# A linear-attention layer and a Fourier mixer on one core: transposes on TensorE, heads in pairs, and Fourier transforms folded in half

## The chip, the cores and the metric

The kernel runs on one core of a Trainium2 chip. The metric is the device time of one execution in microseconds (us). The kernel before took 419.92 us in the median of three runs (419.65 to 425.19).

The engines are named as in the profile: PE is TensorE (PEld its weight loads), DVE is VectorE, ACT is ScalarE, POOL is GpSimd, and SP is SyncE, which here only issues DMAs. PSUM is the memory that TensorE writes.

## The reference

```
# attention: B=4, H=8 heads, S=768 steps, D=48; state is D x D for each head
for t in range(S):
    cur      = outer(u * k[t], v[t])
    y[t]     = r[t] @ (state + cur)
    state    = w[:, None] * state + outer(k[t], v[t])
x = y with the heads side by side                      # B x 768 x 384
# mixer
mixed = real(fft(fft(x, axis=1), axis=2))              # along the sequence, then along the 384 channels
u_    = x + mixed
un    = (u_ - mean(u_)) / sqrt(var(u_) + 1e-6)         # over the 384 channels
out   = u_ + relu(un @ w_ch1) @ w_ch2                  # 384 -> 1536 -> 384
```

## The kernel before, in words

The sequence of a batch is cut into six chunks of 128 steps. Decay powers are folded into r and k (r times w to the power of the position, k times its inverse), so that inside a chunk the attention is two products and a mask: A = k r^T, masked by a triangle (`MA`), then y = MA^T v plus r times the state. The state is 48 x 48 for each head and goes from chunk to chunk.

`phase1_pro(b)` prepares a whole batch. It loads k and r by head on SP's queue and v on ACT's queue, in pieces of 128 x 6 x 48. For each head it scales six chunks at once on DVE (L162, L167) and turns them around by a DMA transpose (L164, L169: r and k, 32 transposes each in the kernel). The term with u (`T1`, `DELTA`, `TTALL`, L171 to L178) is made on DVE for the whole batch in five operations of 2,304 elements a partition.

`phase1_loop(b)` runs over the six chunks: eight matmuls A of one head each (L207, 48 rows of the array), two mask multiplies (L210), sixteen matmuls y (L224 and L227), eight state updates (L233), and on DVE the decay of the state (L239, L242) and the eviction of y into `XSBb` (L244).

`phase2(b)` is the mixer. The transform along the sequence is 12 groups of six matmuls of 384 columns (L274: six row blocks, cosine and sine), each evicted on ACT (L277) and transposed by DMA (L283). The transform along the channels is six groups of six matmuls (L291, L294). For each row block DVE adds x (`UF`, L296) and takes statistics (L297, L298); then one square root and one reciprocal for all six blocks (L300, L301), six normalisations (`UN`, L304), and six DMA transposes (L308). The two layers of the MLP follow: 72 matmuls (L314) with ReLU on ACT (L317), 72 matmuls (L321), and on DVE the residual (`osb`, L324), stored by SP (L325).

The order on each engine is set by a scheduler of the framework, which takes the program in the order in which it is written, with tile pools that say how many buffers each name has, and mixes independent work. The program order is attention 0, tables and weights, and then, for b = 1 to 3, `phase1_pro(b)`, `phase2(b-1)`, `phase1_loop(b)`, and last `phase2(3)`. Each engine runs its own list in order and waits by semaphores for the others.

Of the kernel before, what the change touches and what calls it, by code (L numbers as in the profile page):

```python
# [9 lines left out]
AluOp = mybir.AluOpType  # L11
Act = mybir.ActivationFunctionType
AX = mybir.AxisListType

B = 4
H = 8
# [5 lines left out]
NC = S // L  # L22
DP = 64
# [3 lines left out]
def kernel(  # L27
# [7 lines left out]
    moe_w_ch1: bass.AP,  # L35
    moe_w_ch2: bass.AP,
    out: bass.AP,
    debug: dict | None = None,
    subset: str | None = None,
):  # L40
    nc = tc.nc
    debug = debug or {}

    def dbg_store(name, src_ap):
        if name not in debug:
            return
        dst = debug[name]
        if dst.dtype == src_ap.dtype:
            nc.sync.dma_start(out=dst, in_=src_ap)
        else:  # L50
            nc.gpsimd.dma_start(out=dst, in_=src_ap)
# [12 lines left out]
    _cs_np = np.cos(2.0 * np.pi * np.outer(_n, _n) / S).astype(np.float32)
    _ss_np = np.sin(2.0 * np.pi * np.outer(_n, _n) / S).astype(np.float32)
    _d = np.arange(DM)
    _cd_np = np.cos(2.0 * np.pi * np.outer(_d, _d) / DM).astype(np.float32)
    _nsd_np = (-np.sin(2.0 * np.pi * np.outer(_d, _d) / DM)).astype(np.float32)
    _cs_l = _cs_np.reshape(6, 128, S).transpose(1, 0, 2).astype(mybir.dt.np(mybir.dt.bfloat16))
    _ss_l = _ss_np.reshape(6, 128, S).transpose(1, 0, 2).astype(mybir.dt.np(mybir.dt.bfloat16))  # L70
    _cd_l = _cd_np.reshape(3, 128, DM).transpose(1, 0, 2).astype(mybir.dt.np(mybir.dt.bfloat16))
    _nsd_l = _nsd_np.reshape(3, 128, DM).transpose(1, 0, 2).astype(mybir.dt.np(mybir.dt.bfloat16))
    _mtri_l = _mtri_np.astype(mybir.dt.np(mybir.dt.bfloat16))
    cs_c = nc.inline_tensor(np.ascontiguousarray(_cs_l), name="cs_c")
    ss_c = nc.inline_tensor(np.ascontiguousarray(_ss_l), name="ss_c")
    cd_c = nc.inline_tensor(np.ascontiguousarray(_cd_l), name="cd_c")
    nsd_c = nc.inline_tensor(np.ascontiguousarray(_nsd_l), name="nsd_c")
    mtri_c = nc.inline_tensor(np.ascontiguousarray(_mtri_l), name="mtri_c")
    cs_t = constp.tile([128, 6, S], mybir.dt.bfloat16, name="cs_t")
    ss_t = constp.tile([128, 6, S], mybir.dt.bfloat16, name="ss_t")  # L80
    cd_t = constp.tile([128, 3, DM], mybir.dt.bfloat16, name="cd_t")
    nsd_t = constp.tile([128, 3, DM], mybir.dt.bfloat16, name="nsd_t")
    mtri = constp.tile([128, 128], mybir.dt.bfloat16, name="mtri")
    nc.sync.dma_start(out=mtri, in_=mtri_c.ap())
    def load_big_tables():
        for nb in range(6):
            nc.sync.dma_start(out=cs_t[:, nb, :], in_=cs_c.ap()[:, nb, :])
            nc.sync.dma_start(out=ss_t[:, nb, :], in_=ss_c.ap()[:, nb, :])
        for nb in range(3):
            nc.sync.dma_start(out=cd_t[:, nb, :], in_=cd_c.ap()[:, nb, :])  # L90
            nc.sync.dma_start(out=nsd_t[:, nb, :], in_=nsd_c.ap()[:, nb, :])
    dbg_store("dbg_cst0", cs_t[:, 0, 0:256])
    dbg_store("dbg_cdt0", cd_t[:, 0, 0:256])

    wrow = buildp_obj.tile([128, H, D], mybir.dt.float32, name="wrow")
    nc.sync.dma_start(out=wrow, in_=w.partition_broadcast(128))
    urow = constp.tile([128, H, D], mybir.dt.float32, name="urow")
    nc.scalar.dma_start(out=urow, in_=u.partition_broadcast(128))
    lw = buildp_obj.tile([128, H, D], mybir.dt.float32, name="lw")
    nc.scalar.activation(lw, wrow, Act.Ln)  # L100
    tmp_wp = buildp_obj.tile([128, H, D], mybir.dt.float32, name="tmp_wp")
    wpp = constp.tile([128, H, D], mybir.dt.bfloat16, name="wpp")
    wpn = constp.tile([128, H, D], mybir.dt.bfloat16, name="wpn")
    wpl = constp.tile([128, H, D], mybir.dt.bfloat16, name="wpl")
    nc.vector.tensor_scalar(out=tmp_wp, in0=lw, scalar1=icol[:, 0:1], scalar2=None, op0=AluOp.mult)
    nc.scalar.activation(wpp, tmp_wp, Act.Exp)
    ncol = buildp_obj.tile([128, 1], mybir.dt.float32, name="ncol")
# [27 lines left out]

    if subset == "phase0":
        return

    XSB = []

    def bq(tab):
        return tab.unsqueeze(2).to_broadcast([128, H, NC, D])

# [235 lines left out]
```

## Time and profile before

| | |
|---|---|
| median of three runs | 419.92 us |
| span of the profiled execution (first to last instruction) | 417.7 us |
| mean granted TensorE clock | 0.837 |
| busy PE / DVE / ACT / POOL | 289.8 / 189.8 / 85.2 / 44.5 us |
| first of the 72 first-layer matmuls of batch 0 | 134.15 us |
| last eviction `osb` of batch 3 | 414.23 us |
| DMA packets, of these under 512 bytes | 166,342, 158,000 |

The profile gives no other time for the profiled execution than its span. The median of the runs is 2.2 us above the span.

In a row of the windows view stand the stretch, its length, then busy time and number of instructions of PE, PEld, DVE, ACT and POOL, the granted clock, the DMA engines' busy share and GB/s. In a row of the chain or the timeline stand start, length, engine and operation. In a row of a group stand line, engine, operation, tiles, shapes and count, then busy time and the mean ns of one, then the idle time before it and what ended that.

### The profile page before, as it was taken

The page shows a single profiled execution, that of the slowest core. Times are in us where ns is not written, and L with a number is a line of the kernel's source. Part 1 is how long each engine was busy: PE and PEld are TensorE (multiplying, and loading weights), DVE is VectorE, ACT ScalarE, POOL GpSimd, SP SyncE. Part 2 cuts the span into 40 slices and gives each one's busy share as a digit, 9 for nine tenths or more (in the row PEclk, how much of TensorE's full clock was granted, in tenths as well). Part 3 has the DMA queues.
Part 4 walks back from the last instruction along what each step waited for, and adds up shares of the span by engine and source line. Part 5 has one row for each costly group of instructions (what it writes and reads, how often), then busy time and mean ns, then how long its engine had stood idle before and what let it go on. Part 6 is the DMA issues. An engine that isn't in the chain of part 4 may idle for free. (4 is left out here: it accounts for less than half of the span.)

```text
span 417.7 us, 4723 instructions
## 1 busy us (share of the span) xinstructions
PE 289.8 (69%) x1712; PEld 160.9 (39%) x1712; DVE 189.8 (45%) x326; ACT 85.2 (20%) x161; POOL 44.5 (11%) x95
## 2 busy tenths in 40 slices
PE   0000189885275999865777999866758999982796
PEld 0000046442043556532345456433334565550453
DVE  0244865754565923764168714733571135035012
ACT  3300000312000460211200550320104600220460
POOL 2524400111110000121100000211000000000000
PEclk9999999988585699788755799788866995797799
DMA  8999999355796002466894002547320020131002
GB/s 183 231 192 193 257 224 230 87 118 112 148 220 139 13 19 96 79 135 133 165 189 100 16 36 79 119 105 132 61 48 11 19 96 0 39 75 40 17 20 94
DMA packets 166342, 44.59 MB, mean 107 GB/s; under 512 B 158000, under 2 KB 166320, under 8 KB 166320
## 3 DMA queue, kind: packets, MB, share of 16 engines
q1 hardware_dynamic: 137664, 37.02, 40.7%
q10 hardware_dynamic: 25632, 4.92, 6.2%
q0 software_dynamic: 3024, 2.36, 4.0%
q8 instruction: 13, 0.21, 0.2%
q14 instruction: 9, 0.07, 0.0%
HBM read 22.25 MB, written 4.72 MB: 65 GB/s over the span
## 5 line engine op out<-in xcount | busy, mean ns | idle before, releaser
L314 PE MATMUL pfnA<-UNT,W1SB 128*128 128x384 bf16 x288 | 65.9, 364 | 19.2 <-DMA UNT<-UN 19.2
L207 PE MATMUL A_ps<-RWT,KWT 48*128 48x128 bf16 x192 | 25.3, 270 | 63.0 <-DMA KWT<-KWNh 59.8
L317 ACT ACTIVATE HT<-pfnA 128x384 bf16<-128x384 f32 x96 | 47.1, 491 | 62.1 <-PE pfnA L314 60.8
L321 PE MATMUL pfnB<-W2SB,HT 128*128 128x384 bf16 x288 | 56.3, 331 | 0.0
L324 DVE TENSOR_TENSOR osb<-pfnB,UF 128x384 f32<-128x384 f32 x24 | 13.4, 558 | 83.6 <-PE pfnB L321 82.0
L314 PEld LDWEIGHTS <-W1SB 128*128 128x128 bf16 x288 | 29.8, 106 | 47.9 <-issue 34.0
L274 PE MATMUL pfnA<-XSBb,cs_t 128*128 128x384 bf16 x144 | 39.0, 401 | 12.3 <-ACT t3sb L277 9.7
L274 PE MATMUL pfnA<-XSBb,ss_t 128*128 128x384 bf16 x144 | 39.7, 403 | 10.6 <-ACT t3sb L277 10.6
L277 ACT CAST t3sb<-pfnA 128x384 bf16<-128x384 f32 x48 | 22.5, 478 | 109.8 <-PE pfnA L274 34.4
L207 PEld LDWEIGHTS <-KWT 48*128 48x128 bf16 x192 | 15.5, 116 | 70.9 <-DMA KWT<-KWNh 61.5
L210 DVE TENSOR_TENSOR MA<-A_ps,mtri 128x512 bf16<-128x512 f32 x48 | 32.7, 682 | 21.4 <-PE y_ps L224 18.9
L224 PE MATMUL y_ps<-VALL,MA 128*128 128x48 bf16 x192 | 36.5, 211 | 5.2 <-DVE XSBb L244 3.8
L321 PEld LDWEIGHTS <-HT 128*128 128x128 bf16 x288 | 28.2, 99 | 20.0 <-issue 1.4
L294 PE MATMUL pfnB<-nsd_t,T3ST 128*128 128x384 bf16 x72 | 29.0, 403 | 8.0 <-DMA T3ST<-t3sb 8.0
L227 PE MATMUL y_ps<-SALL,RWT 48*128 48x48 bf16 x160 | 33.7, 211 | 0.0
L291 PE MATMUL pfnB<-cd_t,T3CT 128*128 128x384 bf16 x72 | 28.5, 396 | 4.6 <-DVE STS L297 4.6
L166 POOL MEMSET KWNh<- 128x480 bf16 x32 | 15.9, 497 | 144.6 <-DMA KWT<-KWNh 143.5
L162 DVE TENSOR_TENSOR RWNh<-FST,wpp 128x288 bf16<-128x288 f32 x32 | 14.5, 456 | 32.5 <-DMA RWT<-RWNh 29.0
L156 ACT ACTIVATE VALL<-FST 128x2304 bf16<-128x2304 f32 x4 | 8.5, 2122 | 100.9 <-PE y_ps L224 98.2
L296 DVE TENSOR_TENSOR UF<-pfnB,XSBb 128x384 f32<-128x384 f32 x24 | 13.2, 552 | 33.2 <-PE pfnB L294 33.2
L274 PEld LDWEIGHTS <-ss_t 128*128 128x128 bf16 x144 | 16.4, 115 | 28.0 <-issue 23.1
L274 PEld LDWEIGHTS <-cs_t 128*128 128x128 bf16 x144 | 16.2, 114 | 26.7 <-issue 21.6
(45 smaller groups left out, 233.0 us busy)
## 6 DMA issues: line engine op xcount, KB each, us to landing
FST<-in_k_dram SPq DMA_DIRECT2D x32, 144.0 KB, 3.9
FST<-in_v_dram ACTq DMA_DIRECT2D x32, 144.0 KB, 4.1
FST<-in_r_dram SPq DMA_DIRECT2D x32, 144.0 KB, 4.1
out_dram<-osb SPq DMA_DIRECT2D x24, 192.0 KB, 1.9
W1SB<-in_moe_w_ch_dram POOLq DMA_DIRECT2D x9, 128.0 KB, 5.7
W2SB<-in_moe_w_ch_dram POOLq DMA_DIRECT2D x12, 96.0 KB, 6.0
cs_t<-cs_c SPq DMA_DIRECT2D x6, 192.0 KB, 4.0
ss_t<-ss_c SPq DMA_DIRECT2D x6, 192.0 KB, 3.9
```

Source lines behind the costliest of these rows:

```text
L166: nc.gpsimd.memset(KWNh[:, :, D:128], 0.0)
L207: nc.tensor.matmul(A_ps[:, hh * 128:(hh + 1) * 128], lhsT=kwt_q[:, h, :], rhs=rwt_q[:, h, :], start=True, stop=True)
L210: nc.vector.tensor_tensor(out=MA, in0=A_ps.rearrange("j (h i) -> j h i", h=HG), in1=mtri.unsqueeze(1).to_broadcast([128, HG, 128]), op=Alu ...
L224: nc.tensor.matmul(y_ps[:, h * D:(h + 1) * D], lhsT=mas[g][:, hh, :], rhs=VALL[:, h, q, 0:D], start=True, stop=(q == 0))
L227: nc.tensor.matmul(y_ps[:, h * D:(h + 1) * D], lhsT=rwt_q[:, h, :], rhs=SALL[0:D, h, 0:D], start=False, stop=True)
L274: nc.tensor.matmul(t3ps, lhsT=tab[:, nb, kb * 128:(kb + 1) * 128], rhs=XSBb[:, nb, :], start=(nb == 0), stop=(nb == 5))
L277: nc.scalar.copy(t3sb, t3ps)
L291: nc.tensor.matmul(mps, lhsT=T3CT[:, kb, dt, :], rhs=cd_t[:, dt, :], start=(idx == 0), stop=False)
L294: nc.tensor.matmul(mps, lhsT=T3ST[:, kb, dt, :], rhs=nsd_t[:, dt, :], start=False, stop=(dt == 2))
L314: nc.tensor.matmul(gps, lhsT=W1SB[:, dt, ft * 128:(ft + 1) * 128], rhs=UNT[:, sh * 3:(sh + 1) * 3, dt, :], start=(dt == 0), stop=(dt == 2))
L317: nc.scalar.activation(out=HT[:, ft, sh * 384:(sh + 1) * 384], in_=gps, func=Act.Relu)
L321: nc.tensor.matmul(cps, lhsT=HT[:, ft, sb * 128:(sb + 1) * 128], rhs=W2SB[:, ft, :], start=(ft == 0), stop=(ft == 11))
```

## The change

The kernel is written anew. What is computed is the same, up to where it is rounded; how it is divided changes in five places.

1. **Loads by chunk.** k, r and v come in pieces of 128 x 8 x 48 (all heads of one chunk) on SP's queue, in pools of seven buffers each. The seventy-two loads stand on SP ahead of all stores.
2. **Transposes on TensorE.** r and k of two heads (64 columns each, 48 used) are transposed by a matmul against an identity, eight per chunk, into one PSUM tile `tp`. ACT copies them out: k in two copies of half the partitions into a buffer `KB` that has zeros where the other head of the pair would stand, r in one copy.
3. **Paired heads.** A is a matmul with all 128 rows (k of one head with zeros, r of the pair). The state of a pair is 96 columns wide, with a mask `WD` that holds the decay on the diagonal blocks and zero off them; the old state is added in PSUM by a matmul with the identity, and one DVE operation makes the new state.
4. **Folded transforms.** DVE adds and subtracts the two halves of the sequence (`EO`) and of the channels (`XF`), four operations for each of the last three chunks of a batch. The transform along the sequence then has half the rows and is only made for half the frequencies; the others are the mirrored columns (`TR`, a reversed copy on DVE). It comes out with channels on the partitions, so that no transpose is needed before the second transform. 18 matmuls of 384 or 386 columns take the place of 72, and per row block two of 384 and four of 192 columns take the place of six of 384.
5. **Normalisation by row block.** Square root, reciprocal, normalisation and three transposes on TensorE are made in the loop over the row blocks. The term with u moves to POOL (three operations a chunk) with one sum on DVE.

```
+    def attention(b):
...
+        for q in range(NQ):
...
+            nc.sync.dma_start(out=kt, in_=k[b, :, sl, :].rearrange("h p d -> p h d"))
...
+            nc.vector.tensor_tensor(out=KW[:, :, 0:D], in0=kt, in1=wpn, op=AluOp.mult)
+            nc.vector.tensor_tensor(out=RW[:, :, 0:D], in0=rt, in1=wpp, op=AluOp.mult)
+            V = ap_.tile([128, H, D], BF16, name="V")
+            nc.scalar.copy(V, vt)
+            T1 = ap_.tile([128, H, D], F32, name="T1")
+            nc.gpsimd.tensor_tensor(out=T1, in0=rt, in1=kt, op=AluOp.mult)
+            nc.gpsimd.tensor_tensor(out=T1, in0=T1, in1=urow, op=AluOp.mult)
+            DE = ap_.tile([128, H], F32, name="DE")
+            nc.vector.reduce_sum(out=DE, in_=T1, axis=AX.X)
+            TT = ap_.tile([128, H, D], BF16, name="TT")
+            nc.gpsimd.tensor_tensor(out=TT, in0=V, in1=DE.unsqueeze(2).to_broadcast([128, H, D]), op=AluOp.mult)
+            tp = psA.tile([128, 2, NP, 128], BF16, name="tp", bufs=1)
+            for p in range(NP):
+                nc.tensor.transpose(tp[:, 0, p, :], KW[:, 2 * p:2 * p + 2, :].rearrange("t h d -> t (h d)"), ident)
...
+            KB = KBs[i % 2]
+            nc.scalar.copy(KB[0:64, :, 0, :], tp[0:64, 0, :, :])
+            nc.scalar.copy(KB[64:128, :, 1, :], tp[64:128, 0, :, :])
+            RT = ap_.tile([128, NP, 128], BF16, name="RT")
+            nc.scalar.copy(RT, tp[:, 1, :, :])
...
+                    nc.tensor.matmul(A_ps[:, hh, :], lhsT=KB[:, p, hh % 2, :], rhs=RT[:, p, :],
+                                     start=(hh == 0), stop=(hh == 3), skip_group_check=True)
+                MA = ap_.tile([128, 4, 128], BF16, name="MA")
+                nc.vector.tensor_tensor(out=MA, in0=A_ps, in1=mtri.unsqueeze(1).to_broadcast([128, 4, 128]),
+                                        op=AluOp.mult)
...
+            if q > 0:
+                for p in range(NP):
+                    nc.tensor.matmul(y_ps[:, 2 * p:2 * p + 2, :], lhsT=RT[:, p, :], rhs=Sst[:, p, :, :],
+                                     start=(p == 0), stop=False, skip_group_check=True)
+            for h in range(H):
+                nc.tensor.matmul(y_ps[:, h, :], lhsT=MAs[h // 4][:, h % 4, :], rhs=V[:, h, :],
+                                 start=(q == 0 and h == 0), stop=(h == H - 1), skip_group_check=True)
...
+                if q > 0:
+                    nc.tensor.matmul(u_ps, lhsT=ident, rhs=Sst, start=False, stop=True, skip_group_check=True)
+                Sn = ap_.tile([128, NP, 2, D], BF16, name="Sst")
+                nc.vector.tensor_tensor(out=Sn, in0=u_ps, in1=WD, op=AluOp.mult)
+                Sst = Sn
+            nc.vector.tensor_tensor(out=X[:, q, :], in0=y_ps.rearrange("p h d -> p (h d)"),
+                                    in1=TT.rearrange("p h d -> p (h d)"), op=AluOp.add)
+            if q >= 3:
+                n = q - 3
+                nc.vector.tensor_tensor(out=EO[:, 0, n, :], in0=X[:, n, :], in1=X[:, q, :], op=AluOp.add)
...
+    def mixer(b, X, XF):
+        TT = bp.tile([128, 3, 2, 386], BF16, name="TT2")
+        for par in range(2):
...
+            for cb in range(3):
+                ps = psA.tile([128, 2, m], F32, name="mm", bufs=3)
+                for nb in range(3):
+                    nc.tensor.matmul(ps, lhsT=XF[:, par, nb, cb * 128:(cb + 1) * 128], rhs=tab[:, nb, :],
+                                     start=(nb == 0), stop=(nb == 2))
+                nc.scalar.copy(TT[:, cb, :, par:par + 2 * m - 1:2], ps)
...
+            nc.vector.tensor_copy(TR[:, cb, :, :], TT[:, cb, :, 384:0:-1])
...
+        for blk in range(NQ):
+            ps = psA.tile([128, 2, 192], F32, name="mm", bufs=3)
...
+                nc.tensor.matmul(flat, lhsT=cols(1, ri), rhs=tb[:, 192:576], start=(ri == 0), stop=False,
+                                 skip_group_check=True)
...
+            nc.scalar.activation(out=rstd, in_=mv[:, 1:2], func=Act.Sqrt, bias=eps_t[:, 0:1])
+            nc.vector.reciprocal(out=rstd, in_=rstd)
+            UN = ap_.tile([128, DM], BF16, name="UN")
+            nc.vector.tensor_scalar(out=UN, in0=UF[:, blk, :], scalar1=mv[:, 0:1], scalar2=rstd[:, 0:1],
+                                    op0=AluOp.subtract, op1=AluOp.mult)
+            tps = psA.tile([128, 3, 128], BF16, name="mm", bufs=3)
             for dt in range(3):
+                nc.tensor.transpose(tps[:, dt, :], UN[:, dt * 128:(dt + 1) * 128], ident)
+            nc.scalar.copy(UNT[:, :, blk * 128:(blk + 1) * 128], tps)
...
+    st = attention(0)
+    load_tables()
+    for b in range(B):
+        nxt = attention(b + 1) if b + 1 < B else None
+        mixer(b, *st)
+        st = nxt
```

The two MLP loops are the same as before, except that all their PSUM tiles come from the pool `mm` (three buffers), which the transforms and the transposes of `UN` use too.

Three places in the lists of the engines. On DVE, in the mixer of batch 3, before (`UF` is the sum with x, `STS` and `MV` are the statistics, `RSTD` the inverse deviation of all six blocks, `UN` the normalised block):

```order
L297 BN_STATS STS<-UF 128x6
L296 TENSOR_TENSOR UF<-pfnB,XSBb 128x384
L298 BN_AGGR MV<-STS 128x2
L297 BN_STATS STS<-UF 128x6
L298 BN_AGGR MV<-STS 128x2
L301 RECIPROCAL RSTD<-RSTD 128x6
L304 TENSOR_SCALAR UN<-UF,MV,RSTD 128x384 x6
```

And in the change, at the same place:

```order
L279 TENSOR_TENSOR UF<-mm,X 128x2x192
L282 BN_STATS st<-UF 128x6
L284 BN_AGGR mv<-st 128x2
L287 RECIPROCAL rstd<-rstd 128x1
L289 TENSOR_SCALAR UN<-UF,mv,rstd 128x384
L279 TENSOR_TENSOR UF<-mm,X 128x2x192
```

The reciprocal and the normalisation now stand inside each block, ahead of the next block's sum.

On PE, in the same mixer before, where the second transform ends (`T3CT` and `T3ST` are the transposed results of the first, `W1SB` the weights of the MLP):

```order
L291 LDWEIGHTS T3CT
L291 MATMUL pfnB<-cd_t,T3CT 128x384
L294 LDWEIGHTS T3ST
L294 MATMUL pfnB<-nsd_t,T3ST 128x384
L314 LDWEIGHTS W1SB
L314 MATMUL pfnA<-UNT,W1SB 128x384
```

In the change, between the first and the second row block of that mixer (`TT_2884` is the first transform's result):

```order
L293 LDWEIGHTS UN
L293 MATMUL mm<-ident,UN 128x128
L273 LDWEIGHTS TT_2884
L273 MATMUL mm<-hid_t,TT_2884 128x384
L275 LDWEIGHTS TT_2884
L275 MATMUL mm<-hid_t,TT_2884 128x192
L277 LDWEIGHTS TT_2884
L277 MATMUL mm<-hid_t,TT_2884 128x192
```

Before, the matmuls of all blocks stand in one run and the MLP follows them; now the transposes of a block's `UN` stand ahead of the next block's matmuls.

On SP, while attention 1 and mixer 0 run side by side, before (`FST` is an input tile, `RWNh` and `KWNh` the scaled r and k of a head, `t3sb` a result of the first transform):

```order
L283 DMA_TRANSPOSE T3CT<-t3sb 128x3x128
L283 DMA_TRANSPOSE T3ST<-t3sb 128x3x128
L283 DMA_TRANSPOSE T3CT<-t3sb 128x3x128
L150 DMA FST<-in_k_dram 128x6x48
L164 DMA_TRANSPOSE RWT<-RWNh 128x6x128
L169 DMA_TRANSPOSE KWT<-KWNh 128x6x128
```

In the change, the last rows of SP's list:

```order
L175 DMA kt<-in_k_dram 128x8x48
L176 DMA rt<-in_r_dram 128x8x48
L177 DMA vt<-in_v_dram 128x8x48
L310 DMA out_dram<-osb 128x384 x24
```

The transposes are gone from this queue, and all 24 stores stand behind all loads.

More of the change, by code (lines that the diff above doesn't have):

```diff
@@ L34 @@
     u: bass.AP,
-    moe_w_ch1: bass.AP,
-    moe_w_ch2: bass.AP,
+    w1: bass.AP,
+    w2: bass.AP,
     out: bass.AP,
-    debug: dict | None = None,
-    subset: str | None = None,
 ):
     nc = tc.nc
[L42 to L51, printed above, removed]
@@ L83 @@
[L83 to L91, printed above, removed]
@@ L102 @@
[L102 to L107, printed above, removed]
-    nc.vector.tensor_scalar(out=ncol, in0=icol, scalar1=-1.0, scalar2=1.0, op0=AluOp.mult, op1=AluOp.subtract)
@@ new lines @@
+    ncol = cp.tile([128, 1], F32, name="ncol")
+    nc.vector.tensor_scalar(out=ncol, in0=icol, scalar1=-1.0, scalar2=1.0, op0=AluOp.mult, op1=AluOp.subtract)
+    eps_t = cp.tile([128, 1], F32, name="eps_t")
+    nc.vector.memset(eps_t, 1e-6)
+    lw = cp.tile([128, H, D], F32, name="lw")
+    nc.scalar.activation(lw, wrow, Act.Ln)
+    wpp = cp.tile([128, H, D], F32, name="wpp")
+    wpn = cp.tile([128, H, D], F32, name="wpn")
+    nc.scalar.activation(wpn, lw, Act.Exp, scale=ncol[:, 0:1])
+    nc.scalar.activation(wpp, lw, Act.Exp, scale=icol[:, 0:1])
```

416 lines of the change are left out of this document (166 added, 250 removed).

## The prediction

> **What bounds the kernel now.** I read the page first: busy time and slices.
>
> ```profile
> PE 289.8 (69%) x1712; PEld 160.9 (39%) x1712; DVE 189.8 (45%) x326; ACT 85.2 (20%) x161; POOL 44.5 (11%) x95
> PE   0000189885275999865777999866758999982796
> GB/s 183 231 192 193 257 224 230 87 118 112 148 220 139 13 19 96 79 135 133 165 189 100 16 36 79 119 105 132 61 48 11 19 96 0 39 75 40 17 20 94
> ```
>
> No engine is busy throughout; PE does almost nothing in the first five slices of 10.4 us. So I cut the span at the MLPs. Windows view, from the start to the end of batch 0's MLP, and from batch 2's MLP to the end:
>
> ```profile
> 0.00:54.00 54.00, 2.52 (x16) 1.19 (x16) 21.53 (x29) 7.09 (x9) 20.97 (x47) 1.00 1.13 209
> 54.00:134.00 80.00, 55.35 (x341) 31.08 (x341) 49.41 (x85) 9.25 (x15) 8.88 (x19) 0.82 0.78 162
> ...
> 341.70:388.80 47.10, 34.12 (x211) 19.34 (x211) 16.93 (x39) 6.45 (x14) 0.00 (x0) 0.74 0.20 42
> 388.80:417.70 28.90, 25.39 (x141) 13.94 (x141) 3.35 (x6) 11.30 (x23) 0.00 (x0) 0.95 0.11 41
> ```
>
> For 54 us PE has 2.5 us of work. What it waits for stands in the waits view, and the chain of waits gives the last batch:
>
> ```profile
> PE A_ps L207 <- DMA KWT<-KWNh: 59.8, 10, 29.8
> PE pfnA L314 <- DMA UNT<-UN: 19.2, 6, 8.0
> ...
> 356.80 0.57 DVE XSBb L244
> ...
> 363.73 2.92 DMA T3CT<-t3sb
> ...
> 372.09 0.57 DVE UF L296
> ...
> 386.33 2.34 DMA UNT<-UN
> 388.67 0.14 issue
> 388.81 3.03 PE pfnA L314 x9
> ...
> 396.90 1.06 PE pfnA L314 x6
> ...
> 404.10 10.11 PE pfnB L321 x62
> 414.23 0.56 DVE osb L324
> ```
>
> DMA transposes keep PE waiting 60 us at A and 19 us ahead of the MLPs. From the last chunk (356.80) to the MLP (388.81) pass 32 us; the MLP itself, 388.81 to 414.23, is dense: **25.4 us**, and **3.5 us** follow it. Six matmuls of 384 columns take 1.06 us (0.177 each), but the first nine after the idle time 3.03 us (0.337 each): after a pause PE starts at half speed.
>
> **The change, stage by stage.** The transposes' waits go, and with them the reason for the old order, so I build the new time from the new lists rather than subtract. In the change's lists 14 chunks of attention and mixer 0 stand ahead of MLP 0; six chunks and mixer 1 between MLP 0 and 1; four chunks and mixer 2 ahead of MLP 2; mixer 3 alone ahead of MLP 3. The MLPs hold nearly nothing else, so each is taken at 25.4 us: 101.6 for four. The rest is priced from these rows (groups, then timeline):
>
> ```profile
> L210 DVE TENSOR_TENSOR MA<-A_ps,mtri 128x512 bf16<-128x512 f32 x48 | 32.7, 682 | 21.4 <-PE y_ps L224 18.9
> L173 DVE TENSOR_TENSOR T<-FST,urow 128x2304 bf16<-128x2304 f32 x4 | 10.2, 2551 | 0.0
> L166 POOL MEMSET KWNh<- 128x480 bf16 x32 | 15.9, 497 | 144.6 <-DMA KWT<-KWNh 143.5
> L317 ACT ACTIVATE HT<-pfnA 128x384 bf16<-128x384 f32 x96 | 47.1, 491 | 62.1 <-PE pfnA L314 60.8
> ...
> 54.14 0.34 PE L224 MATMUL y_ps<-VALL,MA 128*128 128x48 bf16 x4
> 54.41 0.61 PE L207 MATMUL A_ps<-RWT,KWT 48*128 48x128 bf16 x4
> ...
> 343.51 0.68 DVE L210 TENSOR_TENSOR MA<-A_ps,mtri 128x512 bf16<-128x512 f32 x1
> 344.11 0.54 DVE L242 TENSOR_TENSOR SALL<-ts,upd_ps 48x384 bf16<-48x384 bf16 x1
> ...
> 374.21 0.54 DVE L296 TENSOR_TENSOR UF<-pfnB,XSBb 128x384 f32<-128x384 f32 x1
> 374.67 0.17 DVE L298 BATCH_NORM_AGGREGATE MV<-STS 128x2 f32<-128x6 f32 x1
> ...
> 372.68 0.56 DVE L297 BATCH_NORM_STATS2 STS<-UF 128x6 f32<-128x384 f32 x1
> ...
> 378.54 0.18 DVE L298 BATCH_NORM_AGGREGATE MV<-STS 128x2 f32<-128x6 f32 x1
> 378.75 0.30 ACT L300 ACTIVATE RSTD<-MV,eps_t 128x6 f32<-128x6 f32 x1 [6.33 <-DVE MV L298]
> 379.09 0.19 DVE L301 RECIPROCAL RSTD<-RSTD 128x6 f32<-128x6 f32 x1 [0.37 <-ACT RSTD L300]
> 379.32 2.43 DVE L304 TENSOR_SCALAR UN<-UF,MV,RSTD 128x384 bf16<-128x384 f32 x6
> ```
>
> Back to back, a DVE operation of 384 elements takes 0.46 to 0.47 us (374.21 to 374.67), a mask multiply of 512 takes 0.60 (343.51 to 344.11). A group of four A matmuls takes 0.61 with its tail, of four y matmuls 0.34. A handoff between engines costs about 0.04 us (378.72 to 378.75).
>
> *One chunk.* DVE has k, r, `DE`, state and x at 0.47 and two masks at 0.60: 3.55 us. The loop through the engines goes from four A matmuls (0.61) over two masks (0.60 + 0.68), four y matmuls (0.34), the next chunk's r transposes (eight small matmuls in all; the four of r like the A row, 0.61) and ACT's copy of 512 elements (0.49 x 512/384, about 0.6; a little high or low by its fixed part) back to A: 3.44 us, with five handoffs 3.65. That DVE fits into it with little to spare on in-order queues, I take as **3.9 us**. In the last three chunks of a batch four additions for the fold join DVE, two of them between the masks (0.94): **4.8 us**. ACT's 2.3 us (three copies of 0.6, v at 0.5) and PE lie beside this.
>
> *One row block, alone.* The new order makes this a chain with nothing beside it, twelve of the 24 times: matmuls 0.71 (4 x 384/2 + 2 x 384 columns at 0.177 per 384) or 1.35 (at 0.337), their tail 0.17; sum, statistics, aggregate, root, reciprocal, normalisation 0.56 + 0.56 + 0.18 + 0.30 + 0.19 + 0.47, six handoffs 0.2; three transposes with tail 0.53. That is 3.9 warm, 4.5 cold; PE works a quarter of it, so I take **4.1 us**, 24.6 for six. The old kernel does the roots once for six blocks, but pays 7 us of transposes behind them: here lies no gain.
>
> *Ahead of MLP 0.* The tables end at 11.2 us before (`wpn`), and the first chunk needs them here too:
>
> ```profile
> 10.69 0.52 ACT L110 ACTIVATE wpn<-tmp_wp 128x384 bf16<-128x384 f32 x1 [0.49 <-DVE tmp_wp L109]
> q10 hardware_dynamic: 25632, 4.92, 6.2%
> ```
>
> Start 11.5. Twelve chunks: 6 x 3.9 + 6 x 4.8 = 52, with the first transform of batch 0 (18 matmuls, 3 to 6 us on PE) squeezed in, 3 more; with DVE's list for it (51 us of operations) this is 55 to 58: 58. Then six blocks mixed with 36 other DVE operations: 1.7 of its own, 2.9 of others, 0.4 unfilled, 5.0 each: 30. Last transposes 0.5. Sum **100 us**. Loads hide: a packet of 192 bytes takes 6.2% x 417.7 x 16 / 25,632 = 16 ns on one of 16 engines, a chunk's 3,072 packets 3.1 us, under 3.9; weights and tables come in the same time and the seven buffers cover them. If that cover is gone, a chunk is late by parts of a microsecond.
>
> *Between MLP 0 and 1.* Four chunks whose inputs are ready, 3.3 us each (their 20 DVE operations sum to 11): 13. Six blocks with 23 other DVE operations, 5.0 each: 30. **43 us.** *Ahead of MLP 2:* 13 + 24.6 + 0.6 = **38 us.** *Ahead of MLP 3:* six evictions behind three matmuls each (0.53), 3.2 and a tail of 0.5; the last reversed copy, 768 elements, 0.9 by the slope of L173; 24.6; last copy 0.6: **30 us.**
>
> Sum: 100 + 43 + 38 + 30 + 101.6 + 3.5 = 316; the median lies 2.2 above the span (419.9 against 417.7): **318 us**.
>
> What no row shows: POOL's three operations per chunk. POOL's only compute row is a memset, 0.50 us for 480 elements, 0.4 for 384; the same work on DVE is 0.47. They stay hidden up to 3.9/3 = 1.3 us each, more than twice either row; I cost them at nothing, and the far end is a rival. The additions of the fold are bf16 in and out, which no row is either; nearest is 0.47, taken, and they cannot cost more than the same with f32. Many small operations also repay a fixed part: L173 gives 2.55/6 = 0.43 per chunk where I use 0.47, so 0.04 x 5 x 24 = 5 us of DVE are in the sum as a loss.
>
> **The rivals.**
>
> *Packed additions.* If the bf16 additions and reversed copies run two elements a cycle, each of 60 falls by half its slope (1.08 ns an element by L173 against 0.47): 0.2 us per addition (48), 0.4 per copy (12), 14 us of DVE, of which about 9 lie on the path: 309 us. Against it: no row. The Trainium skill, "VectorE: DVE Perf Modes", section "The perf-mode tier table", gives twice the speed for tensor_tensor with all operands bf16 in SBUF; no run here shows it.
>
> *POOL and DVE in each other's way.* The change puts 72 two-input operations on POOL beside 96 DVE operations that read two SBUF tensors (k, r and the fold). If these take twice 0.47, 45 us come to DVE, 30 of them on the path: 348 us. Before, POOL only writes zeros, so the trace is silent. The Trainium skill, "GPSIMD Engine Reference", section "Specifications", says that GpSimd's SBUF interfaces are shared with VectorE and contend when a DVE instruction has two SBUF inputs; that speaks against this change, and no run here shows it.
>
> *The chunk loop does not overlap.* One PSUM tile `tp` and one `y_ps` serve all chunks. If each chunk waits for the one before, its chain is 0.47 + 1.2 (eight transposes) + 1.8 (three copies) + 0.6 + 1.3 + 0.35 + 0.56 = 6.3: 2 more for 12 chunks and 2.5 for eight, 44 us: 362; half of it 340. For it: ACT has three copies ahead of A. Against: the next chunk's k transposes stand ahead of this one's y.
>
> *Slower.* POOL as the bound of the attention: 72 operations of t from about 8.5 us on, behind them mixer 2 (25), two MLPs (51), mixer 3 (30) and 3.5. Over 428 us needs 8.5 + 72t + 109.5 + 2.2 > 428, t > 4.3 us, nine times the nearest rows. By the Trainium skill, "GPSIMD Engine Reference", section "Performance versus the Vector engine", a two-input add takes 1.96 times VectorE's time; that would be an estimate of 0.9 us, and the sum would stay.
>
> **How the numbers follow.** Forecast 0.55, its own range 300 to 335 (a block at 3.9 or 4.5 is 5 us either way on twelve, stage one 10); packed additions 0.15; contention 0.12; no overlap 0.13; slower 0.02; the rest lies between. The range leaves out the lowest and highest tenth: 296 to 354. A measurement of this kernel tells about 2% from no change (its three runs lie 1.3% apart): faster needs less than 411. All cases but the last are below: faster 0.95, same 0.03, slower 0.02.
>
> **What would show it.** Right: MLPs 25 us long with DVE at six evictions; first-layer matmuls of batch 0 from about 100 us; chunk results 4 to 5 us apart; in mixer 3 the sums (`UF`) 4.1 us apart; POOL operations under 1.3 us; PE no longer waiting for a DMA after 12 us. Wrong: additions of the fold near 0.25 us; k and r products near 0.9 beside POOL; chunk results over 6 us apart, PE waiting for ACT's copies; MLPs stretched because W2 or W1 came late or the clock stayed at 0.337 per matmul, which would add up to 23 us to each.

## The result, and the profile after

The changed kernel takes **329.05 us** in the median of four runs (326.72 to 330.13), the kernel before 419.78 us on the same chip: ratio 0.786, 95% interval 0.781 to 0.790. The forecast was 318 us, with a range of its own of 300 to 335.

The page of the changed kernel: busy time, then PE and DVE by slices of 8.2 us, then the summary of the chain that ended last.

```profile
PE 220.3 (67%) x1616; PEld 145.2 (44%) x1616; DVE 182.4 (56%) x374; ACT 134.9 (41%) x272; POOL 81.6 (25%) x92
PE   0375467653666479996583799944459995446995
DVE  0989598989989780249894502594430124442022
PE 49%; DVE 28%; ACT 7%; DMA 7%; SPq 5%; issue 3%; ACTq 0%; DVEq 0%
```

Of the empty slices of PE at the start only the first is left. From the second to the thirteenth DVE is nearly full instead, with one hole in the fifth. The windows view cuts the span at the first-layer matmuls of batch 0 (119.85) and batch 3 (297.92), and the first stage at the starts of the first and the twelfth chunk's result (17.98 and 81.53); columns as before.

```profile
17.98:81.53 63.55, 37.37 (x359) 28.01 (x359) 55.37 (x95) 25.80 (x50) 38.83 (x40) 0.76 0.97 189
81.53:119.85 38.32, 22.98 (x175) 17.32 (x176) 33.83 (x70) 15.11 (x30) 18.37 (x17) 0.50 0.38 75
119.85:144.60 24.75, 24.75 (x153) 14.75 (x152) 5.47 (x10) 12.19 (x25) 4.39 (x4) 0.95 0.13 44
209.81:243.45 33.64, 15.86 (x130) 9.80 (x128) 21.00 (x55) 9.51 (x21) 0.83 (x1) 0.67 0.02 7
269.49:297.92 28.43, 13.11 (x73) 7.51 (x72) 13.30 (x34) 7.21 (x17) 0.00 (x0) 0.61 0.02 7
297.92:327.80 29.88, 26.07 (x146) 14.84 (x144) 3.34 (x6) 12.19 (x25) 0.00 (x0) 0.90 0.11 40
```

From the first result to MLP 0 DVE works 55.4 of 63.6 us and 33.8 of 38.3 us: it is the bound there. Ahead of MLP 3, where nothing else runs, no engine works even half of the 28.4 us: a chain is the bound. The waits view says what PE waits for now; the 60 us for DMA transposes are gone:

```profile
PE mm L293 <- DVE UN L289: 44.8, 20, 4.3
PE A_ps L208 <- ACT RT L201: 21.3, 14, 4.5
```

PE waits for a block's normalisation (`UN`) to transpose it, 20 times, up to 4.3 us each. The groups view has the operations that no row showed before:

```profile
L180 DVE TENSOR_TENSOR KW<-kt,wpn 128x384 bf16<-128x384 f32 x24 | 21.8, 915 | 0.0
L181 DVE TENSOR_TENSOR RW<-rt,wpp 128x384 bf16<-128x384 f32 x24 | 22.1, 920 | 0.5 <-ACT wpp L118 0.3 <-DMA rt<-in_r_dram 0.2
L185 POOL TENSOR_TENSOR T<-rt,kt 128x384 f32<-128x384 f32 x24 | 27.5, 1144 | 16.8 <-DMA rt<-in_r_dram 12.9 <-DVE DE L188 3.8
L190 POOL TENSOR_TENSOR TT<-V,DE 128x384 bf16<-128x384 bf16 x24 | 20.6, 859 | 111.2 <-DVE X L233 48.2 <-DVE mv L284 27.1 <-DVE rstd L287 19.2
L238 DVE TENSOR_TENSOR EO<-X 128x384 bf16<-128x384 bf16 x12 | 5.6, 468 | 0.0
```

The products of k and r, costed at 0.47 us, take 0.92 in the mean, 0.52 at the shortest and 1.9 at the longest. The timeline shows how. POOL and DVE, rows of the same 3 us:

```profile
43.86 1.08 POOL L190 TENSOR_TENSOR TT<-V,DE 128x384 bf16<-128x384 bf16 x1 [1.56 <-DVE DE L188]
44.90 1.30 POOL L185 TENSOR_TENSOR T<-rt,kt 128x384 f32<-128x384 f32 x1
46.28 1.20 POOL L186 TENSOR_TENSOR T<-T,urow 128x384 f32<-128x384 f32 x1
...
43.90 0.35 DVE L241 TENSOR_TENSOR XF<-EO 128x384 bf16<-128x384 bf16 x1
44.17 1.18 DVE L180 TENSOR_TENSOR KW<-kt,wpn 128x384 bf16<-128x384 f32 x1
45.27 1.35 DVE L181 TENSOR_TENSOR RW<-rt,wpp 128x384 bf16<-128x384 f32 x1
46.54 1.28 DVE L211 TENSOR_TENSOR MA<-A_ps,mtri 128x512 bf16<-128x512 f32 x2
```

Read the ends. POOL's first ends at 44.94, `KW` 0.41 us later at 45.35, POOL's second 0.85 later at 46.20, `RW` 0.42 later at 46.62, POOL's third 0.86 later at 47.48. Each operation ends about its own working time after the other engine's (a product of k or r takes 0.52 us at the shortest, one of POOL 0.99), although it was started earlier: in these rows the two engines alternate, and neither works beside the other. The mask multiplies, one of whose inputs is in PSUM, take 1.28 us for two beside POOL's third, as much as without POOL (1.29 for two in the run without its work). The Trainium skill, "SBUF — State Buffer", section "Who interferes with whom", says so: VectorE with two SBUF inputs and a GpSimd instruction that reads SBUF exclude each other for a whole instruction, and with at most one SBUF input, outside its two-port modes, VectorE doesn't contend. The rows agree with both halves.

Last, the chain of one block in mixer 3 (timeline, the DVE, ACT and PE rows between two sums `UF`) and PE's two rows of MLP 3 in the chain:

```profile
286.58 0.56 DVE L279 TENSOR_TENSOR UF<-mm,X 128x384 f32<-128x384 f32 x1 [1.88 <-PE mm L277]
287.17 0.56 DVE L282 BATCH_NORM_STATS2 st<-UF 128x6 f32<-128x384 f32 x1
...
287.98 0.29 ACT L286 ACTIVATE rstd<-mv,eps_t 128x1 f32<-128x1 f32 x1 [2.21 <-DVE mv L284]
288.51 0.48 DVE L289 TENSOR_SCALAR UN<-UF,mv,rstd 128x384 bf16<-128x384 f32 x1
289.05 0.50 PE L293 MATMUL mm<-ident,UN 128*128 128x128 bf16 x3 [2.51 <-DVE UN L289]
289.34 0.53 PE L273 MATMUL mm<-hid_t,TR 128*128 128x384 bf16 x1
...
290.87 0.56 DVE L279 TENSOR_TENSOR UF<-mm,X 128x384 f32<-128x384 f32 x1 [1.88 <-PE mm L277]
...
298.12 14.16 PE mm L300 x72
312.29 11.71 PE mm L306 x72
```

From sum to sum pass 4.29 us. The next block's matmuls (289.34) stand behind this block's transposes (289.05) on PE's list, so no block overlaps the one before: of the 4.29 us DVE waits 1.88 for PE (the bracket of the row).

### The profile page after: what moved, and what is told of

It reads as the page before. It is cut to its first block, busy times and chain, and to the rows that moved or that the text cites. A ratio compares the mean times of both kernels' runs of the same rounds, so it can differ in the third digit from the quotient of the medians.

```text
span 327.8 us, 4361 instructions
## 1 busy us (share of the span) xinstructions
PE 220.3 (67%) x1616; PEld 145.2 (44%) x1616; DVE 182.4 (56%) x374; ACT 134.9 (41%) x272; POOL 81.6 (25%) x92
## 4 chain that ended last, share of the span: by engine, by line
PE 49%; DVE 28%; ACT 7%; DMA 7%; SPq 5%; issue 3%; ACTq 0%; DVEq 0%
PE mm L300 16%; PE mm L306 14%; DMA vt<-in_v_dram 4%; DVE MA L211 4%; PE mm L273 4%; DVE UF L279 3%; DVE UN L289 3%; DVE st L282 3%; PE mm L293 3%; DVE RW L181 3%; PE A_ps L208 2%; ACT RT L201 2%; SPq L175 2%; PE mm L277 2%; DVE KW L180 2%
## 5 line engine op out<-in xcount | busy, mean ns | idle before, releaser
L300 PE MATMUL mm<-UNT,W 128*128 128x384 bf16 x288 | 54.3, 355 | 0.0
L302 ACT ACTIVATE HT<-mm 128x384 bf16<-128x384 f32 x96 | 46.8, 490 | 6.7 <-PE mm L300 6.5
L190 POOL TENSOR_TENSOR TT<-V,DE 128x384 bf16<-128x384 bf16 x24 | 20.6, 859 | 111.2 <-DVE X L233 48.2
L306 PE MATMUL mm<-W,HT 128*128 128x384 bf16 x288 | 47.5, 326 | 0.0
L300 PEld LDWEIGHTS <-W 128*128 128x128 bf16 x288 | 30.3, 106 | 21.8 <-issue 6.2
L208 PE MATMUL A_ps<-RT,KB 128*128 128x128 bf16 x192 | 21.3, 269 | 21.9 <-ACT RT L201 21.3
L198 ACT COPY KB<-tp 64x512 bf16<-64x512 bf16 x24 | 13.9, 578 | 44.4 <-PE tp L196 42.4
L185 POOL TENSOR_TENSOR T<-rt,kt 128x384 f32<-128x384 f32 x24 | 27.5, 1144 | 16.8 <-DMA rt<-in_r_dram 12.9
L208 PEld LDWEIGHTS <-KB 128*128 128x128 bf16 x192 | 17.1, 121 | 25.4 <-issue 16.4
L186 POOL TENSOR_TENSOR T<-T,urow 128x384 f32<-128x384 f32 x24 | 26.9, 1124 | 1.5
L194 PE MATMUL tp<-ident,KW 128*128 128x128 bf16 x96 | 13.9, 294 | 18.6 <-DVE KW L180 16.0
L183 ACT CAST V<-vt 128x384 bf16<-128x384 f32 x24 | 12.2, 515 | 34.5 <-PE y_ps L220 22.6
L181 DVE TENSOR_TENSOR RW<-rt,wpp 128x384 bf16<-128x384 f32 x24 | 22.1, 920 | 0.5 <-ACT wpp L118 0.3
L180 DVE TENSOR_TENSOR KW<-kt,wpn 128x384 bf16<-128x384 f32 x24 | 21.8, 915 | 0.0
```

Of the source, the lines that this page charges most:

```text
L180: nc.vector.tensor_tensor(out=KW[:, :, 0:D], in0=kt, in1=wpn, op=AluOp.mult)
L181: nc.vector.tensor_tensor(out=RW[:, :, 0:D], in0=rt, in1=wpp, op=AluOp.mult)
L185: nc.gpsimd.tensor_tensor(out=T1, in0=rt, in1=kt, op=AluOp.mult)
L186: nc.gpsimd.tensor_tensor(out=T1, in0=T1, in1=urow, op=AluOp.mult)
L190: nc.gpsimd.tensor_tensor(out=TT, in0=V, in1=DE.unsqueeze(2).to_broadcast([128, H, D]), op=AluOp.mult)
L208: nc.tensor.matmul(A_ps[:, hh, :], lhsT=KB[:, p, hh % 2, :], rhs=RT[:, p, :], start=(hh == 0), stop=(hh == 3), skip_group_check=True)
```

## The experiments

The theory after the result: the first stage came 20 us late because DVE and POOL exclude each other and because weights and tables share the DMA engines with the chunk loads (only the weights are moved in the runs below); the packed additions gave some of it back. The rivals: the chunk loop does not overlap, or the cold clock. A second question is whether the statistics per block are really worth nothing. The stages of all runs, read from the timeline (start of the first-layer matmuls in us). Each ratio is to the kernel before as it ran beside that kernel (medians 419.78 to 422.60 us), so ratios and medians need not rank two close kernels alike:

| kernel | MLP 0 | MLP 1 | MLP 2 | MLP 3 | median us | ratio to before, 95% interval |
|---|---|---|---|---|---|---|
| changed | 119.85 | 185.41 | 243.45 | 297.92 | 329.05 | 0.786 (0.781 to 0.790) |
| no work of POOL in the chunks | 114.89 | 179.53 | 237.22 | 291.65 | 322.99 | 0.762 (0.756 to 0.767) |
| table of k in PSUM, two buffers `mm` | 118.69 | 183.61 | 241.87 | 299.30 | 331.58 | 0.785 (0.780 to 0.789) |
| two buffers `mm` alone | 119.63 | 185.21 | 244.77 | 302.27 | 336.18 | 0.799 (0.794 to 0.804) |
| fold in f32 | 125.28 | 192.68 | 252.91 | 305.52 | 335.96 | 0.794 (0.789 to 0.799) |
| late weights | 113.42 | 180.14 | 237.87 | 292.16 | 323.76 | 0.764 (0.759 to 0.769) |
| no POOL, late weights | 102.88 | 167.51 | 225.19 | 279.63 | 311.29 | 0.736 (0.730 to 0.742) |
| statistics of six blocks together | 98.08 | 154.38 | 207.13 | 245.81 | 275.55 | 0.653 (0.648 to 0.657) |
| the same, late weights | 93.78 | 150.09 | 202.85 | 241.51 | 270.78 | 0.642 (0.639 to 0.645) |
| the same, late weights and u term on DVE | 86.70 | 140.35 | 195.22 | 234.34 | 264.99 | 0.629 (0.627 to 0.632) |

### POOL's work taken out of the chunks

The term with u is left out and v added in its place, so that DVE keeps as many operations.

```
-  nc.gpsimd.tensor_tensor(out=T1, in0=rt, in1=kt, op=AluOp.mult)
-  nc.gpsimd.tensor_tensor(out=T1, in0=T1, in1=urow, op=AluOp.mult)
-  nc.vector.reduce_sum(out=DE, in_=T1, axis=AX.X)
+  nc.vector.reduce_sum(out=DE, in_=rt, axis=AX.X)
-  nc.gpsimd.tensor_tensor(out=TT, in0=V, in1=DE..., op=AluOp.mult)
...
-  nc.vector.tensor_tensor(out=X[:, q, :], in0=y_ps..., in1=TT..., op=AluOp.add)
+  nc.vector.tensor_tensor(out=X[:, q, :], in0=y_ps..., in1=V..., op=AluOp.add)
```

> The changed kernel without POOL's three operations per chunk: the term with u is left out (v is added to y in its place, DE sums r instead of r*k*u), so DVE still makes every operation of before, with the same operands' sizes. Theory (POOL's two-input operations slow DVE's products of two SBUF tensors, KW and RW, from about 0.52 to 0.92 us): KW and RW at 0.52 to 0.56 us in the mean, the first MLP starts 12 to 18 us earlier than in the changed kernel (119.9 us), total 309 to 318 us. Rival A (KW and RW are slow by their own form, f32 tables and an output in pieces of 48): 0.92 us still, total 327 to 331. Rival B (the chunk loop through ACT's copies sets the pace, not DVE): KW and RW fall, but the first MLP moves by under 5 us.

322.99 us, less gained than the 309 to 318 expected, and MLP 0 comes 5.0 us earlier, not 12 to 18. The groups view and ACT's timeline of this run:

```profile
L181 DVE TENSOR_TENSOR RW<-rt,wpp 128x384 bf16<-128x384 f32 x24 | 13.1, 548 | 12.7 <-ACT wpp L118 9.1 <-DMA rt<-in_r_dram 3.6
L180 DVE TENSOR_TENSOR KW<-kt,wpn 128x384 bf16<-128x384 f32 x24 | 12.9, 544 | 0.0
...
17.05 0.51 ACT L183 CAST V<-vt 128x384 bf16<-128x384 f32 x1 [8.67 <-DMA vt<-in_v_dram]
```

The products fall from 0.92 to 0.55 us, and the eleven intervals from the first to the twelfth chunk's result from 63.6 to 50.9 us. That is 12.7 us, though not all of it need be POOL's, since the weights are loaded earlier here. And the first result comes at 29.0 instead of 18.0: DVE waits for loads, its 9.1 us for `wpp` too, since ACT makes `wpp` behind the copy of the first v, which waits 8.7 us for its load. With nothing to compute, POOL issues the six weight loads from 3.9 us on (13.9 in the changed kernel), and the first chunks' loads share the DMA engines with them. Most of the gain went there. By the signs set down before, this is rival B: the products fall and MLP 0 moves by under 5 us (4.96). The run by itself therefore doesn't tell contention from a chunk loop bound elsewhere; the one after next does.

### The weight loads held back

Each weight tile is first written by a small DVE copy that reads the sixth chunk's result, so the loads wait for that. These copies come so late in DVE's list that the loads are issued at 73.1 to 76.5 us, after the eleventh result, and not at the sixth (43.6).

```
+  nc.vector.tensor_copy(W1[0:1, 0, 0:1], X[0:1, 5, 0:1])   # and so for each of the six loads
   nc.gpsimd.dma_start(out=W1[:, dt, :], in_=w1[...])
```

> The changed kernel with the six weight loads on POOL held back until the sixth chunk of batch 0 is done (six copies of one element into the weight tiles from that chunk's result stand ahead of them). Theory (the weight loads, 2.4 MB written, take the DMA engines from the chunk loads: v of the sixth chunk takes 14.4 us to land): that load lands within 7 us, DVE's wait of 3.2 us at 38 us goes, the first MLP starts 3 to 6 us earlier, total 323 to 327 us. Rival (the table loads on SP and the eight-deep queue cause it): the wait stays, total as the changed kernel or later by POOL's wait.

323.76 us, as the theory has it, and 6.4 us earlier at MLP 0, a little more than the 3 to 6 expected, with POOL's work as it was. What it cures stands in the changed kernel's chain of waits and SP's timeline:

```profile
21.14 14.41 DMA vt<-in_v_dram
...
30.42 3.87 SPq L176 DMA_DIRECT2D rt<-in_r_dram  x1
34.34 3.90 SPq L177 DMA_DIRECT2D vt<-in_v_dram  x1
```

The sixth chunk's v takes 14.4 us, where a v load lands in 3.7 in the median, and two of the issues behind it take 3.9 us each. This is the hole in the fifth slice of DVE. With the weights held back the same load lands in 3.9 us; the tables were still loaded early, so what they cost is not shown.

### Both together

The two edits above; again the term with u is left out.

> The term with u is left out (v added in its place, so that GpSimd has no work in the chunks and its three operations per chunk are gone) and the weight loads start only when the sixth chunk's result is there. Theory (the first stage is VectorE-bound; contention of GpSimd with VectorE and the early weight loads are the two things that lengthened it): products of k and r 0.54 to 0.56 us, first chunk result at 18, eleven intervals of 4.4 to 4.6 us, first MLP at 100 to 104 us, total 307 to 313. Rival (the 11 us that the first chunk lost without GpSimd's work were not the weight loads): first MLP stays at 112 to 116 and the total at 320 to 324.

311.29 us, MLP 0 at 102.88, both inside the expectation; the late first chunk of the run without POOL was the weight loads. The windows of this run, first to twelfth result and on to MLP 0:

```profile
16.62:67.87 51.25, 33.00 (x359) 24.82 (x359) 43.03 (x97) 26.14 (x49) 3.35 (x6) 0.75 0.96 197
67.87:102.88 35.01, 18.35 (x174) 14.18 (x175) 29.40 (x74) 15.18 (x30) 0.64 (x1) 0.65 0.80 142
```

DVE works 43.0 us where it worked 55.4, with nearly the same operations (the six small copies are added, and the sum over `DE` reads another input). It is not that DVE waited for POOL's results: its waits in the changed kernel name no operation of POOL. The clock is much as it was in the first of them (0.75 against 0.76), so it is not what lengthened the changed kernel's. Of the 20 us by which MLP 0 came late, 17 are these two causes: 6.4 for the weights, 10.5 for POOL.

### Is it two SBUF inputs? The table of k in PSUM

Of the two alike products, one gets its table from PSUM. To make room for it the matmul buffers `mm` go from three to two; the second kernel has that alone.

```
-  wpn = cp.tile([128, H, D], F32, name="wpn")
+  wpn = psA.tile([128, H, D], F32, name="wpn", bufs=1)
-  ... name="mm", bufs=3     (five places)
+  ... name="mm", bufs=2
```

> The changed kernel with the table wpn, the second factor of KW, kept in PSUM instead of SBUF (one bank, so the pool mm has two buffers instead of three); RW's table stays in SBUF. POOL's work is unchanged. Theory (the slowing needs two SBUF inputs of the DVE operation): KW 0.53 to 0.60 us, RW still 0.8 to 1.0, beside the same POOL work; total 5 to 12 us shorter unless the smaller pool costs as much. Rival A (own form): KW stays 0.92. Rival C (any DVE operation that reads SBUF beside POOL is slowed): KW stays above 0.8.

> The changed kernel with two PSUM buffers instead of three for the matmuls of mixer and MLP, and nothing else: the control for the run with KW's table in PSUM, which needed that. Theory: the MLPs take 27 to 28 us instead of 25.3, mixer blocks little more, total 337 to 342; the table in PSUM then gained 6 to 10 us against this. Rival (the third buffer was worth nothing, so the table in PSUM gained nothing): 326 to 332, MLPs 25 to 26 us.

The groups view of the kernel with the table in PSUM, and then of that with two buffers alone:

```profile
L180 DVE TENSOR_TENSOR KW<-kt,wpn 128x384 bf16<-128x384 f32 x24 | 12.9, 539 | 0.3 <-DMA kt<-in_k_dram 0.3
L181 DVE TENSOR_TENSOR RW<-rt,wpp 128x384 bf16<-128x384 f32 x24 | 22.8, 952 | 0.5 <-ACT wpp L118 0.3 <-DMA rt<-in_r_dram 0.2
```

```profile
L180 DVE TENSOR_TENSOR KW<-kt,wpn 128x384 bf16<-128x384 f32 x24 | 21.9, 919 | 0.0
L181 DVE TENSOR_TENSOR RW<-rt,wpp 128x384 bf16<-128x384 f32 x24 | 20.5, 857 | 0.3 <-ACT wpp L118 0.3
```

In one run, beside the same work of POOL, the product with one SBUF input takes 0.54 us and the one with two 0.95. That settles which operations suffer. The 0.95 hides one operation of 4.60 us; the other 23 take 0.79. DVE and POOL at that place, in the run with the table in PSUM:

```profile
13.84 4.60 DVE L181 TENSOR_TENSOR RW<-rt,wpp 128x384 bf16<-128x384 f32 x1
...
14.03 0.84 POOL L190 TENSOR_TENSOR TT<-V,DE 128x384 bf16<-128x384 bf16 x1
...
16.56 0.98 POOL L186 TENSOR_TENSOR T<-T,urow 128x384 f32<-128x384 f32 x1
```

Four operations of POOL run one behind the other from 14.03 to 17.54, and only then `RW` ends, at 18.44. So the two engines exclude each other, but they need not take turns: here VectorE waited through several in a row.

The times: 331.58 with the table in PSUM, 336.18 for the control, so the table is worth 4.6 us by the medians and about 6 by the ratios, at or below the low end of the 6 to 10 that the control's expectation gave it (the two ran on different chips). The control itself came out just under its 337, and the third `mm` buffer is worth 7.1 us by the medians, 5.6 by the ratios (MLP 0 takes 27.9 us instead of 24.75, last eviction at 147.54). Not all 24 x 0.38 = 9 us of `KW` come back: behind that one `RW` the first chunk's masks wait, and the first result comes 2.5 us later (20.14 for 17.63).

### The fold in f32

```
-  EO = bp.tile([128, 2, 3, DM], BF16, name="EO", bufs=1)
+  EO = bp.tile([128, 2, 3, DM], F32, name="EO", bufs=1)
```

> The changed kernel with the intermediate of the fold, EO, in f32 instead of bf16, so that none of the 48 additions has only bf16 operands. Theory (the bf16 additions run at twice the rate): the four groups of additions go from a median of 0.345 to 0.54 us, more where POOL runs beside them; 48 x 0.2 = 9.6 us of DVE, of which 3 to 8 us show: total 332 to 338 us. Rival (additions lie off the path): same total within 1.5 us.

335.96 us, 6.9 above the changed kernel, as expected. Two of the four additions, in this run:

```profile
L239 DVE TENSOR_TENSOR XF<-EO 128x384 bf16<-128x384 f32 x12 | 7.0, 586 | 0.0
L237 DVE TENSOR_TENSOR EO<-X 128x384 f32<-128x384 bf16 x12 | 7.2, 598 | 0.0
```

In bf16 throughout, and without POOL, the same additions take 0.348 to 0.351 us, 0.27 from start to start. They are packed: the first rival of the prediction held. The additions alone are worth about 7 us; the prediction gave 9 to additions and reversed copies together. Beside POOL they are blocked too (0.468 in the changed kernel), so a packed addition gains less there. The reversed copies are fast too, though no run undoes them: 768 elements take 0.42 us in the mean in the changed kernel, where the prediction's sum has 0.9.

### The statistics of six blocks together

Not a part undone, but the old kernel's way: sums and statistics of six blocks first, one root, one reciprocal, then six normalisations and 18 transposes.

```
-  mv = ap_.tile([128, 2], F32, name="mv"); nc.vector.bn_aggr(out=mv, in_=st)
+      nc.vector.bn_aggr(out=MV[:, blk, :], in_=st)
+  nc.scalar.activation(out=rstd, in_=MV[:, :, 1], func=Act.Sqrt, ...)      # once for six
+  nc.vector.reciprocal(out=rstd, in_=rstd)
+  for blk in range(NQ):                                                    # second loop
       nc.vector.tensor_scalar(out=UN, ..., MV[:, blk, 0:1], rstd[:, blk:blk + 1], ...)
```

> In each mixer all six sums and their statistics are formed first, then one root and one reciprocal for the six blocks, then six normalisations with their transposes. Theory (the chain of each block alone, 4.29 us in the changed kernel, is made of handoffs that six blocks can share): mixer 3 takes 4.2 + 6 x 1.37 (sum, statistics, aggregate) + 0.7 + 6 x 0.5 + 1.2 = 17 us where it took 28.4; the same 11 us go ahead of MLP 2, parts of it ahead of MLP 0 and 1, where the other work of VectorE filled the waits: 3 and 6. Total about 298 (292 to 305). Rival (the prediction's 'here lies no gain': what the shared root saves comes back as transposes and copies behind it): the stage ahead of MLP 3 stays at 26 to 29 us and the total within 323 to 331.

275.55 us: 53.5 us faster than the changed kernel where 31 were expected, and the rival falls. Mixer 3 of this run, DVE's and PE's timeline:

```profile
236.31 1.02 DVE L280 TENSOR_TENSOR UF<-mm,X 128x384 f32<-128x384 f32 x2 [0.28 <-PE mm L278]
...
242.80 0.19 DVE L287 RECIPROCAL rstd<-rstd 128x6 f32<-128x6 f32 x1 [0.37 <-ACT rstd L286]
243.03 2.43 DVE L290 TENSOR_SCALAR UN<-UF,MV,rstd 128x384 bf16<-128x384 f32 x6
...
243.57 2.45 PE L294 MATMUL mm<-ident,UN 128*128 128x128 bf16 x18 [3.92 <-DVE UN L290]
245.81 1.49 PE L301 MATMUL mm<-UNT,W 128*128 128x384 bf16 x4
```

Six sums and statistics take 6.1 us (236.31 to 242.43), the roots 0.6, and then the transposes run right beside the normalisations and end with them. The stage takes 13.7 us (232.09 to 245.81) instead of 28.4. The other stages: MLP 0 starts 21.8 us earlier (two chunks of batch 2, which stood ahead of it, now stand behind it), from there to MLP 1 9.4 us less, to MLP 2 5.0 less although six chunks stand there now and not four, and the four MLPs together 2.9 less. The sum with 14.7 for mixer 3 is 53.8, the difference of the spans (327.8 and 274.0). The expectation missed mostly ahead of MLP 0: it gave 3 us there, because DVE seemed to fill the waits.

The edit does two things at once, and the run doesn't part them. It makes one root and one reciprocal for six blocks, and it takes the transposes out from between the blocks' matmuls on PE's list. In the changed kernel's block of 4.29 us the root and the reciprocal take 0.53 (287.98 to 288.51) and DVE's wait for PE 1.88; DVE's other operations are the same in both kernels. Five times 1.88 is 9.4 of the 14.7 us of mixer 3, five times 0.53 is 2.7. By this estimate the order on PE is the larger part; a kernel with a root for each block but the next block's matmuls ahead of the transposes was not run.

### Together with late weights, and the u term on DVE

The second kernel replaces POOL's two f32 products per chunk by two bf16 products on DVE from `KW` and `RW`, with one row `uw` = u times w.

```
-  nc.gpsimd.tensor_tensor(out=T1, in0=rt, in1=kt, op=AluOp.mult)
-  nc.gpsimd.tensor_tensor(out=T1, in0=T1, in1=urow, op=AluOp.mult)
+  nc.vector.tensor_tensor(out=T1, in0=RW[:, :, 0:D], in1=KW[:, :, 0:D], op=AluOp.mult)
+  nc.vector.tensor_tensor(out=T1, in0=T1, in1=uw, op=AluOp.mult)
```

> Statistics of six blocks together, and weight loads held back until the sixth chunk's result. If the two gains lie in different places they add: 6 us ahead of MLP 0 on top of the batched statistics, total about 292 (286 to 299). If the weights then arrive late for MLP 0, or the batched mixer 0 is bound by VectorE anyway, the sum is that of the batched statistics alone, 298 or more.

> As the version with batched statistics and late weights, but the two GpSimd products of the u term are made by VectorE from the bf16 products KW and RW (with one row u times w), two bf16 operations of 0.35 us. Per chunk VectorE gains 2 x 0.38 us of contention at k and r and pays 0.70: if contention is by GpSimd's busy time, k and r fall to 0.55 to 0.65 us (GpSimd's third product stays) and the total stays within 4 us of that version, 288 to 296. If contention came from something else, k and r stay near 0.9 and the total rises by 0.7 x 20 = 14 us.

270.78 us: holding the weights back is worth 4.8 us here too, of it 4.3 ahead of MLP 0; the base was faster than the expectation had it. With the u term on DVE 264.99 us, 5.8 less, a little more than the 4 allowed for. Groups of the last kernel:

```profile
L189 DVE TENSOR_TENSOR KW<-kt,wpn 128x384 bf16<-128x384 f32 x24 | 14.3, 601 | 0.0
L190 DVE TENSOR_TENSOR RW<-rt,wpp 128x384 bf16<-128x384 f32 x24 | 13.5, 561 | 0.0
L194 DVE TENSOR_TENSOR T<-RW,KW 128x384 bf16<-128x384 bf16 x24 | 8.9, 371 | 0.1
L199 POOL TENSOR_TENSOR TT<-V,DE 128x384 bf16<-128x384 bf16 x24 | 23.9, 998 | 141.7 <-DVE DE L197 83.4 <-DVE X L242 37.0 <-ACT RT L210 13.4
```

DVE does 48 more operations, and its busy time falls from 172.5 to 168.0 us: two products of 0.37 cost less than the blocking they end. This kernel beats the changed one by 19% (264.99 against 329.05) and the one before by 37%.

## Why the prediction was right and wrong

**The MLPs.** Right: 25.4 each, 101.6 in all; measured 24.75, 24.4, 26.04 and 26.1, in all 101.3.

**Ahead of MLP 0.** Here the forecast failed: 100 us, measured 119.85. The twelfth chunk's result was due at 69.5 and ended at 82.1; the six mixed blocks were due in 30.5 and took 37.7. Two terms were at fault. "I cost them at nothing", of POOL's three operations per chunk: POOL had the time, as argued (0.86 to 1.14 us each in the mean, under 1.3), but what they do to DVE was priced only in a rival, at 30 us on the path; it is 10.5 ahead of MLP 0 and 12.5 in all (323.76 to 311.29). And "weights and tables come in the same time and the seven buffers cover them", with parts of a microsecond if not: it was 6.4 us. The per-chunk sum stands as a total: without these two causes the twelfth result ends at 68.4 and MLP 0 begins at 102.88. As a total only, since 20 additions in it cost 0.2 us less than taken: about 4 us of other time, which the runs do not resolve, stand in their place. The remaining 3 us lie in the mixed blocks (34.5 us for 30.5, begun 1.1 earlier).

**The fold at 0.47 us.** Too high: 0.27 from start to start, worth 7 us. Two of the rivals were therefore partly true at once, with opposite signs, and both of the prediction's signs for them came (additions near 0.25, products of k and r near 0.9). That the forecast lay as close as it did is in part luck: its largest term was 20 us off, and smaller errors went the other way. The third, a chunk loop without overlap, is out: the first to twelfth result take 51 us without the two causes, 4.7 each, where it asked for 6.3.

**The mixer blocks.** A block alone, 4.1 us, measured 4.29; PE was at the slow rate (0.53 for one matmul of 384 columns, which takes 0.33 in the MLPs), the case that the prediction put at 4.5. "Between MLP 0 and 1" 43, measured 40.8. "Ahead of MLP 2" 38, measured 33.6: the four chunks ahead of the first sum took 9.0 us and not 13, since DVE had made their products of k and r before the MLP ahead of them began. "Ahead of MLP 3" 30, measured 28.4. These three are 8 us below the forecast and hid part of the first stage's 20.

**"Here lies no gain."** The most expensive sentence. It set the six roots against the old kernel's 7 us of DMA transposes behind them, as if these came with the roots. They don't: with TensorE transposes and the statistics of six blocks together the MLP starts 0.35 us after the last normalisation (245.46 to 245.81), and the chain of 4.29 us per block becomes 1.0 for the statistics and 0.4 for normalisation and transposes. This sentence bears on what the change could have been, so the forecast did not suffer from it.

The sum again: 316 predicted for the span, + 19.9 ahead of MLP 0, - 8.2 in the three stages between, - 0.3 in the MLPs, + 0.3 at the end, is the measured 327.8.

## What to carry to other kernels

Before moving elementwise work to GpSimd, look at the inputs of what VectorE does meanwhile: with two in SBUF the two engines shut each other out here, and two packed bf16 products on VectorE were cheaper than handing the same work over. Where a chain of small steps runs once per block, ask which of them can be done for all blocks together, what stands between the blocks on each engine's in-order list, and price it with the new kernel's operations, not with the old one's. And a load hidden by the average rate is not hidden where a large one that isn't needed yet is issued ahead of it.

## What was unexpected of the hardware

- GpSimd and VectorE shut each other out for whole instructions: a product of 384 f32 took 0.52 to 1.9 us on VectorE (once 4.60, behind four operations of GpSimd), and GpSimd's own 0.99 when nothing blocked it, 1.14 in the mean. With one input in PSUM VectorE's product stayed at 0.54.
- An addition of 384 bf16 elements took 0.35 us, 0.27 from start to start; beside POOL's work it took 0.38 to 0.47, and 0.59 to 0.77 with an f32 side. The Trainium skill, "VectorE: DVE Perf Modes", section "The perf-mode tier table", cited in the prediction as a rival, gives twice the speed for this form; from start to start it was 1.7 times here (0.27 against 0.47).
- A 192 KB load that lands in 3.7 us in the median took 14.4 us with weight and table loads in flight, and 3.9 with the weights held back.
